# Digit comparisons stored by groups of four token columns, the first expert's high parts first, and a new plan, in a fused attention and routing kernel

## The chip, the cores and the metric

The program runs on one core of a Trainium2 chip. The metric is the device time of one execution in microseconds (us). Before the change it was 493.65 us as the median of three runs (492.44 to 495.6).

## The reference

Attention over 4 batches, 8 heads, 768 positions and 64 features: four sink keys and a window of 128, softmax, product with v. Its output is read as 3072 tokens of 512 features, and a greedy routing sends each token to one of 8 experts:

```python
cap = N // E                                   # 3072 / 8 = 384
logits = x @ w_gate
for idx in np.argsort(-logits.flatten()):      # best pairs first
    tok, e = idx // E, idx % E
    if assigned[tok] >= 0 or counts[e] >= cap: continue
    assigned[tok] = e; counts[e] += 1
for e in range(E):
    mask = assigned == e
    h = np.maximum(x[mask] @ w1[e], 0.0)       # 512 -> 1024
    out[mask] = h @ w2[e]                      # 1024 -> 512
```

Every expert gets exactly 384 tokens, and its MLP is done with float32 accuracy.

## The kernel before, in words

**Stages.** Attention takes the first 139 us, token columns of 128 tokens each (24 columns, NC=24). Then `Moe` runs eight rounds. Round k has a routing phase `Rk` (`phase`), which finds the expert that fills up next and its 384 tokens; a gather of these rows out of DRAM (`rows`, L683), which also transposes them on TensorE (L691) and splits them into a high part `xh` (ScalarE, L693) and a low part `xl` (VectorE, L694); the loading of the expert's 4 MB of weights as 8 pieces of 512 KB on SyncE's queue (`weights`, L674), each split into `wh` (ScalarE, L676) and `wl` (VectorE, L678); and the MLP (`mlp`).

**The MLP.** A product is made of three: high by high, high by low, low by high. Each of the 8 slices f of the hidden layer takes 4 x 3 matmuls of 384 columns (L704), then ScalarE and VectorE split the result into `hh` and `hl` (L707, L708). The second layer takes 3 x 8 x 3 matmuls of 512 columns (L716).

**A routing phase.** A token's best logit is turned into a sortable integer, and its digits are searched from the top in six steps (`STEPS`): two of 64 digit values (m=64), four of 32 (m=32). In a step VectorE compares the digits of all 24 columns with the m values (`compare`, L497, tile `cmp`), and TensorE counts per expert with one product for each group of columns: the weights are 128 columns of `cmp`, the moving operand is the one-hot `oh` (L567, 12 products of 128x16 for m=64, 6 of 128x32 for m=32). VectorE turns the counts into a digit (L584 to L589), one product with a constant matrix (L593) spreads it, VectorE takes the step's threshold from it (L595, L596), and the next step begins. After the six steps, ranks come from two products (L614, L615), and the tokens' indices from one more comparison and 12 products (`pick`, L640). The routing of round k+1 runs among the MLP products of round k; `R0` has nothing to run among. In `R0` and while the first rows are gathered, products with a constant (`warm`, L543) run in between.

**How `cmp` lies.** Before, a value of `cmp` is at `[digit value][token column]`: the 128 columns that one product loads as weights are `NC*m/128` elements apart, 12 elements (24 bytes) for m=64 and 6 elements (12 bytes) for m=32.

**What sets the order.** `graph` lists the work items with an engine and a cost, `order` is a list scheduler with one bias per class of items (`BIAS`: R, X, M, W and so on for each round) and a window (`WIN`), and `run` writes the instructions down in that order. Each engine works through its own list strictly in this order, so an item that is not ready holds back what stands behind it on its engine. The costs are the planner's own and set the order only.

Of the kernel before, what the change touches and what calls it, by code (L numbers as in the profile page):

```python
# [385 lines left out]
class Graph:  # L386
# [18 lines left out]
    def order(self,bias,win,free):  # L405
# [44 lines left out]
class Moe:  # L450
# [40 lines left out]
    def part(self,j,m): return self.cmp[j][:,0:m*NC].rearrange("p (x c) -> p x c",x=128)  # L491
    def compare(self,j,xb,m,a,b,op=OP.is_ge,dt=BF):

        V=self.nc.vector; g=128//m; h=NC//g
        o=self.part(j,m).bitcast(dt).rearrange("p (j m) c -> p j m c",j=g); x=xb.rearrange("p (j c) -> p j c",j=g)[:,:,None,:].to_broadcast([128,g,m,h])
        r=self.grid[:,None,0:m,0:h].to_broadcast([128,g,m,h])
        if (a,b)==(0,NC): V.tensor_tensor(o,x,r,op); return  # L497
        for i in range(g):
            c,d=max(a,i*h)-i*h,min(b,i*h+h)-i*h
            if c<d: V.tensor_tensor(o[:,i,:,c:d],x[:,i,:,c:d],r[:,i,:,c:d],op)  # L500
    def prep(self,k,a,b):

# [15 lines left out]
            (u(8*n),lambda: V.tensor_tensor(self.oh[:,c],w,wide(mx),OP.is_equal),'w1 mx','oh'),  # L518
            (u(32*n),lambda: self.compare(0,self.xb0,64,a,b),'xb0','cmp0'),
            (u(n/2),lambda: V.tensor_scalar(di[:,1],s,-2**31,15,op0=OP.bitwise_xor,op1=OP.logical_shift_right),'s','di1'),  # L520
# [24 lines left out]
    def phase(self,g,k):  # L545
# [7 lines left out]
        if not last:  # L553
# [79 lines left out]
        ip,bn=bank()  # L633
        v(u(NC*32),lambda: self.compare(oj,self.lo,64,0,NC,OP.is_equal,F16),'lo',on)
        v(u(6*NC),lambda: V.tensor_tensor(R,c4[:,:,0:6],c4[:,:,1:7],OP.subtract),'c40 c4','R')
        v(u(6*NC),lambda: V.tensor_tensor(self.R3,R,self.tid[:,:,None].to_broadcast([128,NC,6]),OP.mult),'R','R3')
        def pick():
            if first: self.warm(ip,WARM[6])
            OH=self.part(oj,64).bitcast(F16); h=NC//2
            for c in range(h): nc.tensor.matmul(ip[:,0:12],OH[:,:,c],self.R3.rearrange("p (j c) g -> p c j g",j=2)[:,c],start=c==0,stop=c==h-1)  # L640
        e(12*62*slow,pick,on+' R3',bn,'ip')

# [37 lines left out]
    def rows(self,g,k):  # L680
# [5 lines left out]
        for c in range(4):  # L686

            tp,tn=(self.py[c%2],f'py{c%2}') if k==0 and c>1 else (self.pt[c%2],f'pt{c%2}')
            pts=[tn,tn+'.1',tn+'.2']
            for t in range(3):  # L690
                g.add('E',110,lambda t=t,c=c,tp=tp: nc.tensor.transpose(tp[:,128*t:128*t+128],self.xg[t][:,128*c:128*c+128],self.idn),  # L691
                      [f'xg{t}'],[pts[t]],f'X{k}.{c}.{t}',f'X{k}')
            g.add('A',371,lambda c=c,tp=tp: nc.scalar.activation(self.xh[b][:,c,:],tp[:,0:CAP],AF.Copy),pts,[f'xh{b}.{c}'],f'xh{k}.{c}',f'X{k}')  # L693
            g.add('V',469,lambda c=c,tp=tp: nc.vector.tensor_tensor(self.xl[b][:,c,:],tp[:,0:CAP],self.xh[b][:,c,:].bitcast(F32),OP.subtract),pts+[f'xh{b}.{c}'],[f'xl{b}.{c}'],f'xl{k}.{c}',f'X{k}')  # L694

    def mlp(self,g,k):
        nc=self.nc; b=k%2; cls=f'M{k}'; idx=self.idx[k]
# [35 lines left out]
    def run(self):  # L733
# [113 lines left out]
```

## Time and profile before

| | |
|---|---|
| median of 3 runs | 493.65 us |
| the profiled execution | 495.15 us, span 493.4 us |
| TensorE matmuls busy | 454.1 us, 92% of the span |
| VectorE busy | 363.5 us, 74% |
| ScalarE / GpSimd busy | 225.5 us / 159.4 us |
| mean granted TensorE clock | 0.964 |

The profile is of one execution. Busy time counts an engine's instructions from first to last moment; matmuls are pipelined, so one matmul's duration is longer than the step from one start to the next. PEld stands for TensorE's weight loads, DVE for VectorE, ACT for ScalarE, POOL for GpSimd, SPq for SyncE's queue.

### The profile page before, as it was taken

Reading aid. Unit: us, or ns where it says so; the run is one execution under the profiler, and the core shown is the slowest. Engines: PE = TensorE matmul, PEld = TensorE weight load, DVE = VectorE, ACT = ScalarE, POOL = GpSimd, SP = SyncE. Lnnn points to the kernel's source line nnn. Section 1 sums busy time; section 2 is a strip of 40 time slices with the busy share of each in tenths; the row PEclk is TensorE's granted clock in tenths of the full one; section 3 lists DMA queues with packets and bytes.
Section 4 is the critical chain, followed back from the end, with each engine's and each line's share of the span. In section 5 each row is a group of like instructions: output and inputs, shape, how many; then the busy total and the mean of one; then the engine's idle time right before and its main releaser. Section 6 shows DMA issues by size and latency. Waiting matters only on the chain.

```text
span 493.4 us, 14321 instructions
## 1 busy us (share of the span) xinstructions
PE 454.1 (92%) x5572; PEld 377.8 (77%) x5572; DVE 363.5 (74%) x1168; ACT 225.5 (46%) x667; POOL 159.4 (32%) x322
## 2 busy tenths in 40 slices
PE   8799999988764989999999899999999999999994
PEld 4587877777632678788878778887988988998983
DVE  5799999989956877997888877986977764622010
ACT  5887888878300351541622442640632355612120
POOL 5877878767710300410320311201021303100011
PEclk9899999999955889999999999999999999999999
DMA  8766767752210570930922912902921995100011
GB/s 278 245 190 200 226 216 215 210 166 93 88 44 9 154 245 0 324 146 28 348 74 73 333 44 80 361 10 83 322 65 43 328 345 181 45 0 23 21 43 44
DMA packets 44452, 73.28 MB, mean 149 GB/s; under 512 B 3424, under 2 KB 20960, under 8 KB 44384
## 3 DMA queue, kind: packets, MB, share of 16 engines
q1 hardware_dynamic: 39968, 59.11, 36.2%
q0 software_dynamic: 3840, 12.59, 7.2%
q8 instruction: 44, 0.72, 0.6%
q10 hardware_dynamic: 576, 0.67, 0.5%
q14 instruction: 24, 0.20, 0.1%
HBM read 59.77 MB, written 12.58 MB: 147 GB/s over the span
## 4 chain that ended last, share of the span: by engine, by line
PE 57%; DVE 19%; DMA 9%; ACT 6%; issue 4%; POOL 2%; SPq 0%; POOLq 0%; ACTq 0%; DVEq 0%
PE py L716 22%; PE ph L704 20%; DMA raw<-w 7%; ACT P L24 4%; PE pp L83 3%; PE pr L567 3%; DVE nmx L95 2%; PE pp L132 2%; DVE wl L678 2%; PE pt L691 2%; DVE xt L149 2%; PE pp L112 2%; DVE at L139 1%; PE pp L143 1%; PE pp L145 1%
## 5 line engine op out<-in xcount | busy, mean ns | idle before, releaser
L676 ACT ACTIVATE wh<-raw 128x1024 fp32r<-128x1024 f32 x64 | 67.7, 1061 | 83.8 <-DVE fin L654 33.5
L678 DVE TENSOR_TENSOR wl<-raw,wh 128x1024 fp32r<-128x1024 f32 x64 | 77.4, 1217 | 27.4 <-ACT wh L676 27.0
L704 PE MATMUL ph<-xh,wh 128*128 128x384 f32 x256 | 90.7, 354 | 0.2 <-DVE hl L708 0.2
L704 PE MATMUL ph<-xl,wh 128*128 128x384 f32 x256 | 86.8, 339 | 0.0
L704 PE MATMUL ph<-xh,wl 128*128 128x384 f32 x256 | 86.8, 339 | 0.0
L683 POOL DMA_INDIRECT xg<-x_dram,idx x24 | 30.4, 1268 | 156.1 <-issue 37.8
L716 PE MATMUL py<-wh,hh 128*128 128x512 f32 x192 | 79.2, 413 | 0.0
L24 ACT ACTIVATE P<-pp,nmx 128x128 f32<-128x128 f32 x192 | 68.5, 379 | 16.1 <-DVE nmx L97 14.2
L716 PE MATMUL py<-wl,hh 128*128 128x512 f32 x192 | 75.4, 393 | 0.0
L716 PE MATMUL py<-wh,hl 128*128 128x512 f32 x192 | 75.4, 393 | 0.0
L721 POOL DMA_INDIRECT out<-yo,idx x24 | 24.9, 1037 | 137.0 <-ACT yo L719 122.7
L707 ACT ACTIVATE hh<-ph 128x384 fp32r<-128x384 f32 x64 | 30.7, 486 | 71.9 <-PE ph L704 55.3
L708 DVE SCALAR_TENSOR_TENSOR hl<-ph,hh 128x384 fp32r<-128x384 f32 x64 | 35.1, 552 | 30.3 <-ACT hh L707 29.5
L704 PEld LDWEIGHTS ph<-xh,wh 128*128 128x128 f32 x256 | 49.1, 192 | 5.6 <-issue 2.9
L704 PEld LDWEIGHTS ph<-xl,wh 128*128 128x128 f32 x256 | 48.7, 190 | 2.1 <-DVE xl L694 0.3
L704 PEld LDWEIGHTS ph<-xh,wl 128*128 128x128 f32 x256 | 48.5, 189 | 0.0
L83 PE MATMUL pp<-kk,q 64*64 64x204 f32 (+2 forms) x768 | 42.7, 333 | 3.5 <-ACT P L24 2.0
L716 PEld LDWEIGHTS py<-wh,hl 128*128 128x128 f32 x192 | 36.0, 188 | 8.1
L24 ACT ACTIVATION_READ_ACCUMULATOR P<-pp,nmx 128x1 f32 x192 | 41.7, 217 | 0.0
L716 PEld LDWEIGHTS py<-wh,hh 128*128 128x128 f32 x192 | 36.7, 191 | 6.1 <-issue 1.3
L118 POOL TENSOR_TENSOR E<-PT,me 128x256 f32<-128x256 f32 x48 | 35.4, 753 | 15.0 <-ACT PT L24 14.9
L716 PEld LDWEIGHTS py<-wl,hh 128*128 128x128 f32 x192 | 36.2, 189 | 4.3
(161 smaller groups left out, 794.9 us busy)
## 6 DMA issues: line engine op xcount, KB each, us to landing
raw<-w SPq DMA_DIRECT2D x64, 512.0 KB, 7.4
kk<-kd SPq DMA_DIRECT2D x23, 272.0 KB, 3.7
v<-vd SPq DMA_DIRECT2D x24, 256.0 KB, 3.1
x_dram<-xt SPq DMA_DIRECT2D x24, 256.0 KB, 3.4
q<-qd SPq DMA_DIRECT2D x22, 256.0 KB, 3.7
xg<-x_dram,idx POOLq DMA_INDIRECT x24, 6.0
out<-yo,idx POOLq DMA_INDIRECT x24, 2.7
us<-ud SPq DMA_DIRECT2D x1, 288.0 KB, 5.3
```

The costliest lines, as they stand in the source:

```text
L24: def act(*a,**k): last[:]=[nc.scalar.activation(*a,**k)]
L83: PE.matmul(sp[o,s,204*u+a:204*u+204],q[p,2*g+u,o],kk[p,2*i-2+f+a//68:2*i+f+1,2*g+u],start=True,stop=True)
L118: def op_A(c,g): G.tensor_tensor(T('E',c)[:,2*g:2*g+2],diag(c,g),me[:,None].to_broadcast([128,2,2,64]),OP.mult)
L567: nc.tensor.matmul(cnt[:,0:z*E],self.part(j,m)[:,:,c],self.oh.rearrange("p (j c) e -> p c j e",j=z)[:,c],start=c==0,stop=c==h-1)
L676: g.add('A',947,lambda wh=wh,raw=raw: nc.scalar.activation(wh,raw,AF.Copy),[f'raw{q}'],[f'wh{s}'],f'H{k}.{j}',f'W{k}')
L678: g.add(e,{'V':1160,'P':2303}[e],lambda wh=wh,wl=wl,raw=raw,e=e: (nc.vector if e=='V' else nc.gpsimd).tensor_tensor(wl,raw,wh.bitcast(F32) ...
L683: g.add('P',1350,lambda t=t: nc.gpsimd.indirect_dma_start(out=self.xg[t],out_offset=None,in_=self.x_dram,in_offset=bass.IndirectOffsetOnAx ...
L704: nc.tensor.matmul(p[:,0:CAP],x[:,c,:],y[:,c,:],start=c==0 and i==0,stop=c==3 and i==2)
L707: g.add('A',371,lambda f=f,p=p: nc.scalar.activation(self.hh[:,f,:],p[:,0:CAP],AF.Relu),ps,[f'hh{f}'],f'hh{k}.{f}',f'H{k}')
L708: g.add('V',469,lambda f=f,p=p: nc.vector.scalar_tensor_tensor(self.hl[:,f,:],p[:,0:CAP],0.0,self.hh[:,f,:].bitcast(F32),op0=OP.max,op1=OP ...
L716: nc.tensor.matmul(p,x[:,f,ts],w,start=f==0 and i==0,stop=f==7 and i==2)
L721: st=nc.gpsimd.indirect_dma_start(out=self.out,out_offset=bass.IndirectOffsetOnAxis(ap=idx[:,t:t+1],axis=0),in_=y,in_offset=None)
```

## The change

`RUN` gives the number of token columns in a group, 4 in all eight rounds. `compare` now writes `cmp` as `[group of 4][digit value][column in the group]`, so the columns that a product loads as weights are 4 elements (8 bytes) apart, and VectorE's operands run over 4 elements at a time. `gather` issues the products, for counting and for `pick` alike. For m=64 there are 12 products as before. For m=32 there are 8 in place of 6: four of 128 weights, and four of 64, as 24 columns make six groups and a product of 128 weights takes four of them. In the first round, slices 0 and 1 of the hidden layer take the eight matmuls with `xh` first and the four with `xl` at the end, and the counting of step 1 of `R1` is put behind the first two of these items (`m0go`). Costs of the planner, its window and all biases are new.

```diff
+RUN=[4]*8
...
-                if k and tiny: c+=90
+                if k and tiny: c+=15
...
-    def compare(self,j,xb,m,a,b,op=OP.is_ge,dt=BF):
+    def compare(self,j,xb,m,a,b,k,op=OP.is_ge,dt=BF):
-        V=self.nc.vector; g=128//m; h=NC//g
+        V=self.nc.vector; g=128//m; h=NC//g; U=RUN[k]
+        if U:
+            a//=U; b//=U; n=b-a
+            o=self.cmp[j][:,0:m*NC].bitcast(dt).rearrange("p (t m u) -> p t m u",m=m,u=U)[:,a:b]
+            x=xb[:,U*a:U*b].rearrange("p (t u) -> p t u",u=U)[:,:,None,:].to_broadcast([128,n,m,U])
+            V.tensor_tensor(o,x,self.grid[:,None,0:m,0:U].to_broadcast([128,n,m,U]),op); return
...
+    def gather(self,out,j,m,y,k,dt=BF):
+
+        z=128//m; U=RUN[k]; n=y.shape[2]; l=[]
+        if U:
+            for b in range(0,NC//U,z):
+                q=min(z,NC//U-b)
+                st=self.cmp[j][:,b*m*U:(b+q)*m*U].bitcast(dt).rearrange("p (x u) -> p u x",u=U); mv=y[:,b*U:(b+q)*U].rearrange("p (j u) e -> p u j e",u=U)
+                l+=[(q*m,q*n,st[:,u],mv[:,u]) for u in range(U)]
+        else:
+            st=self.part(j,m).bitcast(dt); mv=y.rearrange("p (j c) e -> p c j e",j=z)
+            l=[(128,z*n,st[:,:,c],mv[:,c]) for c in range(NC//z)]
+        l=[l[0]]+[x for x in l if x[0]<128]+[x for x in l[1:] if x[0]==128]
+        for i,(r,w,a,b) in enumerate(l): self.nc.tensor.matmul(out[0:r,0:w],a,b,start=i==0,stop=i==len(l)-1)
...
-                    for c in range(h):
-                        nc.tensor.matmul(cnt[:,0:z*E],self.part(j,m)[:,:,c],self.oh.rearrange("p (j c) e -> p c j e",j=z)[:,c],start=c==0,stop=c==h-1)
-                e(h*slow*62,counts,cn+' oh',bn,f'cnt{n}')
+                    self.gather(cnt,j,m,self.oh,k)
+                e({0:62*h if m==64 else 52*h,2:27*h,4:29*h if m==64 else 250}[RUN[k]]+(100 if first else 0),counts,cn+' oh'+(' m0go' if (k,n)==(1,1) else ''),bn,f'cnt{n}')
...
-                def mm(c=c,p=p,wh=wh,wl=wl):
+                def mm(c=c,p=p,wh=wh,wl=wl,two=k==0 and f<2):
+                    if two:
+                        for i,x in enumerate((wh,wl)): nc.tensor.matmul(p[:,0:CAP],x[:,c,:],self.xh[b][:,c,:],start=c==0 and i==0,stop=False)
+                        return
...
+            if k==0 and f<2:
+                for c in range(4): g.add('E',174,lambda c=c,p=p,wh=wh: nc.tensor.matmul(p[:,0:CAP],wh[:,c,:],self.xl[b][:,c,:],start=False,stop=c==3),[f'xl{b}.{c}',pn+('.3' if c==0 else f'.l{c-1}')],[pn+f'.l{c}'],f'Ml{f}.{c}',cls)
+                ps+=[pn+f'.l{c}' for c in range(4)]
...
-            if s-te>340 and te>=tr: ex.append((te+1,int((s-te-170)//165)))
+            if s-te>340 and te>=tr: ex.append((te+1,max(0,int((s-te-600)//165))))
...
-WIN=[33, 1401090, 1049]
+WIN=[110, 2865394, 2192]
...
```

The plan moves items on all engines. Three places are shown, the numbers of instructions left out.

TensorE, one counting of m=32 in `R0`, and the product that spreads its digit. Before:

```order
L567 MATMUL pr0_3339<-oh_106,cmp1_110 128x32
L567 LDWEIGHTS cmp1_110
L567 MATMUL pr0_3339<-oh_106,cmp1_110 128x32
L567 LDWEIGHTS cmp1_110
L567 MATMUL pr0_3339<-oh_106,cmp1_110 128x32
L593 LDWEIGHTS wt1_70
L593 MATMUL pr0_3339<-i81_112,wt1_70 128x8
```

The same place now:

```order
L519 MATMUL pr0_3338<-oh_106,cmp1_110 64x16
L519 LDWEIGHTS cmp1_110
L519 MATMUL pr0_3338<-oh_106,cmp1_110 64x16
L519 LDWEIGHTS cmp1_110
L519 MATMUL pr0_3338<-oh_106,cmp1_110 128x32
L519 LDWEIGHTS cmp1_110
L519 MATMUL pr0_3338<-oh_106,cmp1_110 128x32
L519 LDWEIGHTS cmp1_110
L519 MATMUL pr0_3338<-oh_106,cmp1_110 128x32
L611 LDWEIGHTS wt1_70
L611 MATMUL pr0_3338<-i81_112,wt1_70 128x8
```

Behind a first product of 128 weights come the four of 64 and then the other three of 128.

TensorE where the first MLP begins (`py1` holds the last transposed rows, `cmp1` is step 1 of `R1`). Before:

```order
L567 MATMUL pr0_3339<-oh_106,cmp1_110 128x16
L691 MATMUL py1_3338<-idt_62,xg2_3322 128x128
L704 MATMUL ph0_3334<-xh0_3323,wh0_3296 128x384
L704 MATMUL ph0_3334<-xl0_3325,wh0_3296 128x384
L704 MATMUL ph0_3334<-xh0_3323,wl0_3308 128x384
```

Now:

```order
L708 MATMUL py1_3337<-idt_62,xg2_3321 128x128
L721 MATMUL ph0_3333<-xh0_3322,wh0_3295 128x384
L721 MATMUL ph0_3333<-xh0_3322,wl0_3307 128x384
L721 MATMUL ph0_3333<-xh0_3322,wh0_3295 128x384
L721 MATMUL ph0_3333<-xh0_3322,wl0_3307 128x384
L721 MATMUL ph1_3334<-xh0_3322,wh0_3295 128x384
L721 MATMUL ph1_3334<-xh0_3322,wl0_3307 128x384
L519 LDWEIGHTS cmp1_110
L519 MATMUL pr0_3338<-oh_106,cmp1_110 128x16
```

The 12 countings of step 1 have gone from in front of the last transposed rows to behind six matmuls of the MLP.

VectorE around step 2 of `R1`, between its comparison and its digit `i81`, on which TensorE's L593 (now L611) waits. Before:

```order
L497 TENSOR_TENSOR cmp0_109<-xb0_103,grid_66 128x768
L576 SCALAR_TENSOR_TENSOR y_96<-x0_101,df_108 128x24
L678 TENSOR_TENSOR wl2_3310<-raw2_3290,wh2_3298 128x1024
L584 TENSOR_SCALAR odd_113<-pr0_3339 64x16
L678 TENSOR_TENSOR wl3_3311<-raw3_3291,wh3_3299 128x1024
L585 TENSOR_TENSOR two_114<-pr0_3339,odd_113 64x16
L588 TENSOR_SCALAR odd_113<-two_114 32x8
L678 TENSOR_TENSOR wl4_3312<-raw4_3292,wh4_3300 128x1024
L589 SCALAR_TENSOR_TENSOR i81_112<-two_114,odd_113 32x8
```

Now (`wl2` stands three instructions ahead of the first row):

```order
L500 TENSOR_TENSOR cmp0_109<-xb0_103,grid_66 128x768
L594 SCALAR_TENSOR_TENSOR y_96<-x0_101,df_108 128x24
L732 SCALAR_TENSOR_TENSOR hl0_3327<-ph0_3333,hh0_3326 128x384
L695 TENSOR_TENSOR wl3_3310<-raw3_3290,wh3_3298 128x1024
L602 TENSOR_SCALAR odd_113<-pr0_3338 64x16
L732 SCALAR_TENSOR_TENSOR hl0_3327<-ph1_3334,hh0_3326 128x384
L603 TENSOR_TENSOR two_114<-pr0_3338,odd_113 64x16
L695 TENSOR_TENSOR wl4_3311<-raw4_3291,wh4_3299 128x1024
L606 TENSOR_SCALAR odd_113<-two_114 32x8
L695 TENSOR_TENSOR wl5_3312<-raw5_3292,wh5_3300 128x1024
L607 SCALAR_TENSOR_TENSOR i81_112<-two_114,odd_113 32x8
```

Before, the comparison stood ahead of `wl2` and the digit behind `wl4`; now the comparison stands behind `wl2` and the digit behind `wl5`.

## Rows read from the trace of the kernel before

**Rows 1.** The page: busy time of TensorE, and its granted clock in 40 slices.

```profile
PE 454.1 (92%) x5572; PEld 377.8 (77%) x5572; DVE 363.5 (74%) x1168; ACT 225.5 (46%) x667; POOL 159.4 (32%) x322
...
PEclk9899999999955889999999999999999999999999
```

**Rows 2.** Stretches: start and end, length, busy time by engine, granted clock, DMA.

```profile
139.00:161.00 22.00, 10.88 (x82) 5.77 (x83) 14.41 (x80) 0.00 (x0) 0.67 (x3) 0.50 0.09 28
...
178.00:181.00 3.00, 0.58 (x5) 0.35 (x4) 2.14 (x6) 2.09 (x4) 0.00 (x0) 1.00 1.01 382
181.00:184.20 3.20, 3.20 (x17) 2.89 (x17) 2.71 (x8) 2.93 (x4) 0.00 (x0) 0.51 0.12 44
...
340.00:380.00 40.00, 40.00 (x252) 34.61 (x252) 32.14 (x116) 14.34 (x21) 5.84 (x6) 1.00 0.44 151
```

**Rows 3.** Chain of waits in `R0`: start, length, what.

```profile
143.47 0.91 DVE cmp L497
...
144.43 0.88 PE pr L567 x12
...
160.04 0.84 PE pr L640 x12
```

**Rows 4.** Timeline of TensorE inside trains: start, length, engine, line, operation, count.

```profile
168.03 0.38 PE L567 MATMUL pr<-oh,cmp 128*128 128x16 bf16 x4
...
174.82 0.34 PE L567 MATMUL pr<-oh,cmp 128*128 128x32 bf16 x4
...
197.18 0.20 PE L614 MATMUL pr<-M,ltf 128*128 128x48 bf16 x1
...
197.22 0.18 PE L615 MATMUL pr<-sc,onesb 128*128 128x48 bf16 x1
...
197.25 0.49 PE L716 MATMUL py<-wh,hh 128*128 128x512 f32 x1
```

**Rows 5.** Costliest groups: busy us, mean ns of one, idle before.

```profile
L704 PEld LDWEIGHTS ph<-xh,wl 128*128 128x128 f32 x256 | 48.5, 189 | 0.0
...
L83 PEld LDWEIGHTS pp<-kk,q 64*64 64x64 f32 x768 | 25.2, 134 | 9.6 <-ACT P L24 2.8 <-DMA q<-qd 1.4 <-ACT PT L24 0.8
L567 PE MATMUL pr<-oh,cmp 128*128 128x16 bf16 (+1 forms) x336 | 25.1, 204 | 4.2 <-DVE cmp L497 2.6 <-DVE di L523 1.3
```

**Rows 6.** Timeline of VectorE: comparisons of three sizes in `R0`.

```profile
141.49 0.44 DVE L500 TENSOR_TENSOR cmp<-xb,grid 128x192 bf16<-128x192 bf16 x1
...
143.41 0.96 DVE L497 TENSOR_TENSOR cmp<-xb,grid 128x1536 bf16<-128x1536 bf16 x1
...
146.36 0.56 DVE L497 TENSOR_TENSOR cmp<-xb,grid 128x768 bf16<-128x768 bf16 x1
```

**Rows 7.** Waits of TensorE from 171 us on: total us, times, longest.

```profile
PE pr L593 <- DVE i L589: 3.5, 3, 2.4
PE pr L567 <- DVE cmp L497: 1.2, 2, 0.7
```

**Rows 8.** Timeline of TensorE around its longest wait in the first MLP.

```profile
177.91 0.33 PE L704 MATMUL ph<-xl,wh 128*128 128x384 f32 x1
178.09 0.34 PE L704 MATMUL ph<-xh,wl 128*128 128x384 f32 x1
180.84 0.17 PE L593 MATMUL pr<-i,wt 128*128 128x8 bf16 x1 [2.42 <-DVE i L589]
...
181.15 0.52 PE L704 MATMUL ph<-xl,wh 128*128 128x384 f32 x1
181.47 0.52 PE L704 MATMUL ph<-xh,wl 128*128 128x384 f32 x1
```

**Rows 9.** Timeline of VectorE in the same stretch.

```profile
175.63 1.23 DVE L678 TENSOR_TENSOR wl<-raw,wh 128x1024 fp32r<-128x1024 f32 x1 [1.14 <-ACT wh L676]
...
179.50 1.23 DVE L678 TENSOR_TENSOR wl<-raw,wh 128x1024 fp32r<-128x1024 f32 x1 [0.79 <-ACT wh L676]
180.64 0.15 DVE L589 SCALAR_TENSOR_TENSOR i<-two,odd 32x8 bf16<-32x8 f32 x1
```

**Rows 10.** Timeline of ScalarE: the high parts of weight pieces 4 and 5.

```profile
178.41 1.06 ACT L676 ACTIVATE wh<-raw 128x1024 fp32r<-128x1024 f32 x1 [1.35 <-DMA raw<-w]
...
180.72 1.06 ACT L676 ACTIVATE wh<-raw 128x1024 fp32r<-128x1024 f32 x1 [0.50 <-DMA raw<-w]
```

More of the change, by code (lines that the diff above doesn't have):

```diff
@@ L518, in prep @@
             (u(8*n),lambda: V.tensor_tensor(self.oh[:,c],w,wide(mx),OP.is_equal),'w1 mx','oh'),
-            (u(32*n),lambda: self.compare(0,self.xb0,64,a,b),'xb0','cmp0'),
+            (u((32,32,64,32,32)[RUN[k]]*n),lambda: self.compare(0,self.xb0,64,a,b,k),'xb0','cmp0'),
             (u(n/2),lambda: V.tensor_scalar(di[:,1],s,-2**31,15,op0=OP.bitwise_xor,op1=OP.logical_shift_right),'s','di1'),
@@ L561, in phase @@
                 cnt,bn=bank(); j=n%2; cn=f'cmp{j}'; z=128//m; h=NC//z
-                if n: v(u(NC*m/2),lambda j=j,m=m: self.compare(j,xb[j],m,0,NC),f'xb{j}',cn)
+                if n: v(u(NC*m/(1 if RUN[k]==2 else 2)),lambda j=j,m=m: self.compare(j,xb[j],m,0,NC,k),f'xb{j}',cn)
                 def counts(n=n,m=m,cnt=cnt,z=z,h=h,j=j):
                     if first: self.warm(cnt,WARM[n])
-                    for c in range(h):
-                        nc.tensor.matmul(cnt[:,0:z*E],self.part(j,m)[:,:,c],self.oh.rearrange("p (j c) e -> p c j e",j=z)[:,c],start=c==0,stop=c==h-1)
-                e(h*slow*62,counts,cn+' oh',bn,f'cnt{n}')
+                    self.gather(cnt,j,m,self.oh,k)
+                e({0:62*h if m==64 else 52*h,2:27*h,4:29*h if m==64 else 250}[RUN[k]]+(100 if first else 0),counts,cn+' oh'+(' m0go' if (k,n)==(1,1) else ''),bn,f'cnt{n}')
                 if n:
@@ L633, in phase @@
         ip,bn=bank()
-        v(u(NC*32),lambda: self.compare(oj,self.lo,64,0,NC,OP.is_equal,F16),'lo',on)
+        v(u(NC*(64 if RUN[k]==2 else 32)),lambda: self.compare(oj,self.lo,64,0,NC,k,OP.is_equal,F16),'lo',on)
         v(u(6*NC),lambda: V.tensor_tensor(R,c4[:,:,0:6],c4[:,:,1:7],OP.subtract),'c40 c4','R')
@@ L638, in pick @@
             if first: self.warm(ip,WARM[6])
-            OH=self.part(oj,64).bitcast(F16); h=NC//2
-            for c in range(h): nc.tensor.matmul(ip[:,0:12],OH[:,:,c],self.R3.rearrange("p (j c) g -> p c j g",j=2)[:,c],start=c==0,stop=c==h-1)
-        e(12*62*slow,pick,on+' R3',bn,'ip')
+            self.gather(ip,oj,64,self.R3,k,F16)
+        e({0:740,2:310,4:350}[RUN[k]]+(100 if first else 0),pick,on+' R3',bn,'ip')
         r2=ip[:,0:12].rearrange("p (j t o) -> p j t o",j=2,o=2); sw=self.sw
@@ L690, in rows @@
             for t in range(3):
-                g.add('E',110,lambda t=t,c=c,tp=tp: nc.tensor.transpose(tp[:,128*t:128*t+128],self.xg[t][:,128*c:128*c+128],self.idn),
+                g.add('E',98,lambda t=t,c=c,tp=tp: nc.tensor.transpose(tp[:,128*t:128*t+128],self.xg[t][:,128*c:128*c+128],self.idn),
                       [f'xg{t}'],[pts[t]],f'X{k}.{c}.{t}',f'X{k}')
@@ L701, in mlp @@
             for c in range(4):
-                def mm(c=c,p=p,wh=wh,wl=wl):
+                def mm(c=c,p=p,wh=wh,wl=wl,two=k==0 and f<2):
+                    if two:
+                        for i,x in enumerate((wh,wl)): nc.tensor.matmul(p[:,0:CAP],x[:,c,:],self.xh[b][:,c,:],start=c==0 and i==0,stop=False)
+                        return
                     for i,(x,y) in enumerate(((wh,self.xh[b]),(wh,self.xl[b]),(wl,self.xh[b]))):
                         nc.tensor.matmul(p[:,0:CAP],x[:,c,:],y[:,c,:],start=c==0 and i==0,stop=c==3 and i==2)
-                g.add('E',522,mm,[f'wh{s}',f'wl{s}',f'xh{b}.{c}',f'xl{b}.{c}']+([pn if c==1 else pn+f'.{c-1}'] if c else []),[pn] if c==0 else [pn+f'.{c}'],f'M{k}.{f}.{c}',cls)
+                two=k==0 and f<2
+                g.add('E',348 if two else 522,mm,[f'wh{s}',f'wl{s}',f'xh{b}.{c}']+([] if two else [f'xl{b}.{c}'])+([pn if c==1 else pn+f'.{c-1}'] if c else []),([pn] if c==0 else [pn+f'.{c}'])+(['m0go'] if (k,f,c)==(0,0,1) else []),f'M{k}.{f}.{c}',cls)
             ps=[pn]+[pn+f'.{c}' for c in (1,2,3)]
+            if k==0 and f<2:
+                for c in range(4): g.add('E',174,lambda c=c,p=p,wh=wh: nc.tensor.matmul(p[:,0:CAP],wh[:,c,:],self.xl[b][:,c,:],start=False,stop=c==3),[f'xl{b}.{c}',pn+('.3' if c==0 else f'.l{c-1}')],[pn+f'.l{c}'],f'Ml{f}.{c}',cls)
+                ps+=[pn+f'.l{c}' for c in range(4)]
             g.add('A',371,lambda f=f,p=p: nc.scalar.activation(self.hh[:,f,:],p[:,0:CAP],AF.Relu),ps,[f'hh{f}'],f'hh{k}.{f}',f'H{k}')
```

2 lines of the change are left out of this document (1 added, 1 removed).

## Prediction

> **What bounds the kernel now.** I read the busy times and the granted clock first [rows 1], then the stretches [rows 2], then the chain of waits in `R0` [rows 3], then TensorE's waits behind it [rows 7], and last the timeline inside the trains of small products [rows 4]. The reader is to see two different kernels. From 139 to 161 us, in `R0`, TensorE is busy half the time at half the clock [rows 2], and the end is set by a chain that hands from VectorE to TensorE and back; a train of 12 counting products takes 0.88 us of it, the train of `pick` 0.84 us [rows 3]. From the first MLP on, TensorE is the bound: 40.00 of 40 us are busy from 340 to 380 us [rows 2], and from 171 us on its waits sum to 4.7 us, all on a routing phase's digit or comparison [rows 7]. There, what a train loses or gains on TensorE comes out of the time nearly one to one. One place is worse than its wait: after 2.4 us without work at 178 us [rows 8] the granted clock is 0.51 for the next 3.2 us, though it was 1.00 up to then [rows 2].
>
> **The change, part by part.** *Spacing of the weights.* Inside a train, four starts at 24 bytes between weight columns span 0.38 us, so one step is (0.38 - 0.204)/3 = 0.059 us, with 204 ns for the last product itself; at 12 bytes it is (0.34 - 0.204)/3 = 0.045 us [rows 4, 5]. Two products whose constant weights lie side by side follow each other, and are followed, within 0.04 and 0.03 us [rows 4], 0.035 on the mean. No row has 8 bytes. The ends are 0.045 (no better than 12 bytes) and 0.030. [...]
>
> [...]
>
> A train of 12 has 11 steps, so it gives back 11 x (0.059 - 0.031) = 0.31 us. From the first MLP on there are 18 of them on TensorE (two in `R1`, three each in `R2` to `R6`, one in `R7`): **5.5 us**. Two more lie on the chain of `R0` (step 1 and `pick`): **0.6 us**. Step 0 of `R0` is mostly done under attention and counts for nothing; if that cover were gone it would cost 0.3 us.
>
> *m=32: eight products for six.* Before, 5 steps of 0.045 = 0.23 us; now 7 steps of 0.031 = 0.22 us. Over 28 trains (24 in `R1` to `R6`, 4 in `R0`) that is **-0.3 us**. The other end, 0.045 a step, is +2.5 us.
>
> *The comparisons.* Even runs of 12 and of 6 elements cost the same: 1536 elements take 0.96 and 768 take 0.56 us, so 0.40 us for 768; a run of three, 192 elements, takes 0.44 us [rows 6]. Runs of four are even, so I take the same rate and no change for the large ones. The last columns of `R0` are now 256 elements in an even run, 0.56 - 512 x 0.40/768 = 0.29 us in place of 0.44: **-0.15 us** on the chain. The other end, half the rate, is a rival below.
>
> *High parts first.* Work is moved, not removed: the train of step 1 of `R1` goes from ahead of the MLP to inside it. The MLP starts earlier by that train and by the wait for the first low parts, and does the train later. Its cover is the weights: pieces 4 and 5 arrive so late that ScalarE starts on them at 178.41 and 180.72 us [rows 10], and VectorE behind it. I cost it at **-0.1 us**, between 0 and -0.6.
>
> *The first MLP in the new order.* Before, `wl4` ran from 179.50 us, the digit of step 2 followed at 180.64 [rows 9], and L593 with all of the MLP behind it waited from 178.09 to 180.84 [rows 8]. Now the digit stands behind `wl5` too: by the same rows ScalarE ends piece 5 at 181.78 [rows 10], `wl5` takes 1.23 more, and the digit comes at 183.0. But TensorE has more MLP products ahead of that L593 now, and it first has to wait for step 2's comparison, which now stands behind `wl2` (from 175.63 for 1.23 us [rows 9]). So I see two waits of about one microsecond in place of one of 2.4: the sum stays, what is late next is again a weight piece, but no stretch is long enough to be followed by the low clock. At half clock a matmul of 384 columns took 0.32 us where it took 0.18 [rows 8]; of the 3.2 us at 0.51 [rows 2] half is given back, **-1.6 us**. Ends: 0 and -1.6 for the clock, -2.4 and +2.4 for the waits.
>
> *The rest of the plan.* The small waits in rounds 2 and 3 (the 2.3 us left of rows 7) may go or double; the tail behind the last product is the same list of instructions. I take **0**, within 2.3 either way.
>
> **Sum:** -5.5 - 0.6 - 0.3 - 0.15 - 0.1 - 1.6 = -8.25 us. The profiled execution took 495.15 us, 1.5 above the median of the runs, 493.65; its span 493.4 leaves 1.75 around it, which stays. Its own sum is 486.9; against the median, which is what will be compared, it is 485.4. **Forecast 485.5 us.**
>
> **The rivals.** *More.* The new order also removes three quarters of TensorE's waits of rows 7, 3.5 us: 481.9 us. For it: two of them are in rounds whose order is new; against it: in the first MLP I read waits again. Chance 0.12.
>
> *Eight bytes bring little.* The excess over side-by-side weights could shrink with the distance alone: 0.024 at 24 bytes, 0.010 at 12, some 0.007 at 8. Then a step is 0.042, trains of 12 give 20 x 11 x 0.017 = 3.7, and m=32 loses 28 x (7 x 0.042 - 0.23) = 1.8: 493.65 - 3.7 + 1.8 - 0.15 - 0.1 - 1.6 = 489.9 us. Chance 0.13. The change would not do what it says.
>
> *Short weights load slowly.* Half as many columns may not load faster: float32 weights of 128 columns take 189 ns, of 64 columns 134 [rows 5], so 64 columns cost 55 ns there. If the four products of 64 step at 0.055, a train for m=32 takes 3 x 0.031 + 4 x 0.055 = 0.31 us, 0.08 more than before: 28 x 0.08 = +2.2 in place of -0.3, and the time is 487.9 us. For it: the change makes such products where there were none; against it: no row has 16-bit weights of 64 columns. Chance 0.10. [...]
>
> *The waits take it back.* If the digit of step 2 is waited for in one piece until 183.0, the clock falls as before and the first MLP gains nothing but the 0.1; if the other waits double too (+2.3), the time is 485.4 + 1.6 + 2.3 = 489.3 us. Chance 0.12.
>
> *Slower: the comparisons lose half their rate.* [...] On the chain of `R0` that is 2 x 0.80 + 4 x 0.40 = 3.2 us in full. In `R1` to `R6` it is 3 x 0.8 + 4 x 0.4 = 4.0 each, 24 in all, of which MLP products cover part; at half of it the time is 485.4 + 3.2 + 12 = 500.6 us. It decides (over 498.6) once some 10 of the 24 us show. Against it: 12 and 6 elements cost the same rate; for it: three did not. Chance 0.06.
>
> **How the numbers follow.** The forecast itself, from 482.5 to 488, has 0.47. About 1%, 4.9 us, is what a measurement of this kernel can tell from no change. Faster by over 1% is below 488.7: the forecast, "more" and about half of the short weights, 0.64. Slower by over 1% is above 498.6: the comparisons and a plan that fits badly somewhere, 0.09. The rest is 0.27. The range takes in the middle rivals and most of "more", 480.5 to 493.
>
> **What would show it.** Right: in the new trace, steps of some 0.031 us inside the trains of 12, which then span some 0.55 us in place of 0.84 to 0.88; comparisons still 0.96 and 0.56 us; granted clock 1.00 from the first MLP on; TensorE's waits on L611 and L519 no more than 4.7 us. Wrong: steps of 0.045 and up, trains for m=32 above 0.3 us, comparisons above 1 us, a low clock at the first MLP (it is kept up by fewer `warm` products now), or a new wait of several microseconds in a later round, where a weight piece stands ahead of a digit on VectorE.

## The result, and the profile after

The changed kernel takes 502.62 us (median of four runs, 500.15 to 504.48), the one before beside it 494.62 us: ratio 1.0145, 95% interval 1.0102 to 1.0187. It is slower, by some 7 to 8 us, where the forecast was 485.5. The profiled execution took 504.48 us and is the longest of the four.

The page of the changed kernel: busy time, and TensorE's granted clock in 40 slices. They answer to [rows 1].

```profile
PE 457.7 (91%) x5621; PEld 379.6 (76%) x5621; DVE 364.0 (72%) x1167; ACT 225.0 (45%) x667; POOL 159.7 (32%) x322
...
PEclk9899999999975899959999999999999999999998
```

TensorE is busy for 3.6 us longer, in 49 products more, though its trains of 12 are shorter. In the clock, the 15th slice (from 173 us before, 176 us now) went from 8 to 9, and the 18th (from 214 us) fell from 9 to 5.

Stretches of the changed kernel, with the columns of [rows 2]: TensorE's busy time is the first after the length, the granted clock the third number from the end.

```profile
172.00:178.00 6.00, 5.75 (x44) 5.00 (x41) 4.99 (x13) 3.50 (x6) 0.00 (x0) 1.00 0.80 269
178.00:184.00 6.00, 5.43 (x34) 4.68 (x33) 4.93 (x10) 4.75 (x8) 0.00 (x0) 1.00 0.70 258
208.00:212.00 4.00, 4.00 (x19) 3.13 (x18) 3.65 (x10) 2.53 (x3) 0.99 (x1) 1.00 1.06 403
212.00:216.00 4.00, 1.57 (x18) 1.04 (x17) 2.77 (x5) 1.54 (x2) 0.99 (x1) 0.94 1.04 384
216.00:220.00 4.00, 2.15 (x14) 1.26 (x13) 2.73 (x12) 0.81 (x3) 0.44 (x1) 0.50 0.40 147
220.00:224.00 4.00, 3.68 (x20) 3.34 (x21) 3.46 (x11) 2.92 (x6) 0.54 (x1) 0.50 0.19 70
```

The first MLP (172 to 184 us) runs at full clock, as forecast, and TensorE pauses in it for 0.8 us in all where two waits of about one were forecast. The long wait and the low clock stand 35 us later instead: from 212 to 220 us TensorE works 3.7 of 8 us, and it is at half clock from 216 us on.

The timeline of TensorE in the changed kernel: a train of the 64-value step in `R0`, one of a 32-value step, and the products around the long wait.

```profile
145.44 0.56 PE L519 MATMUL pr<-oh,cmp 128*128 128x16 bf16 x12 [0.42 <-DVE cmp L500]
...
187.33 0.75 PE L519 MATMUL pr<-oh,cmp 128*128 128x32 bf16 x8
...
212.74 0.56 PE L519 MATMUL pr<-oh,cmp 128*128 128x16 bf16 x12
213.16 0.41 PE L708 MATMUL pt<-idt,xg 128*128 128x128 f32 x2
216.84 0.17 PE L611 MATMUL pr<-i,wt 128*128 128x8 bf16 x1 [3.26 <-DVE i L607]
```

The train of 12 in `R0` takes 0.56 us, 0.32 less than before [rows 3]. But the train of eight is 0.75 us, and each of the 28 is like it (0.72 to 0.79). Six products of before take 0.45 (a row below shows such a train).

VectorE in the changed kernel: the comparisons of two sizes, which answer to [rows 6], and its work during that wait.

```profile
144.42 0.96 DVE L500 TENSOR_TENSOR cmp<-xb,grid 128x1536 bf16<-128x1536 bf16 x1
...
212.76 1.21 DVE L695 TENSOR_TENSOR wl<-raw,wh 128x1024 fp32r<-128x1024 f32 x1
214.00 0.17 DVE L606 TENSOR_SCALAR odd<-pr 64x8 f32<-64x8 f32 x1
215.37 1.22 DVE L695 TENSOR_TENSOR wl<-raw,wh 128x1024 fp32r<-128x1024 f32 x1 [1.20 <-ACT wh L693]
216.62 0.16 DVE L607 SCALAR_TENSOR_TENSOR i<-pr,odd 64x8 bf16<-64x8 f32 x1
...
217.46 0.56 DVE L500 TENSOR_TENSOR cmp<-xb,grid 128x768 bf16<-128x768 bf16 x1
```

The comparisons cost what they did. Routing's digit `i` had its first half (`odd`) at 214.00, but a low part of a weight piece stands between, and that one waits for ScalarE:

```profile
214.28 1.06 ACT L693 ACTIVATE wh<-raw 128x1024 fp32r<-128x1024 f32 x1 [2.47 <-DMA raw<-w]
```

ScalarE waits 2.47 us for the transfer of the piece. So a transfer holds VectorE's queue, that holds `i`, and `i` holds TensorE's whole queue. Waits of TensorE in the changed kernel from 165 us on (total, times, longest), which answer to [rows 7]:

```profile
PE pr L519 <- DVE cmp L500: 4.3, 4, 2.2
PE pr L611 <- DVE i L607: 4.1, 4, 3.3
```

They are 8.4 us where they were 4.7. By themselves they do not make this kernel slower than the one before: an experiment below has as much of them and takes 491 us.

### The profile page after: what moved, and what is told of

Its sections match the earlier page's. It is cut to its first block, busy times and chain, and to the rows that moved or that the text cites. A ratio compares the mean times of both kernels' runs of the same rounds, so it can differ in the third digit from the quotient of the medians.

```text
span 502.7 us, 14432 instructions
## 1 busy us (share of the span) xinstructions
PE 457.7 (91%) x5621; PEld 379.6 (76%) x5621; DVE 364.0 (72%) x1167; ACT 225.0 (45%) x667; POOL 159.7 (32%) x322
## 5 line engine op out<-in xcount | busy, mean ns | idle before, releaser
L724 PE MATMUL ph<-xh,wh 128*128 128x384 f32 x248 | 88.6, 357 | 0.6 <-DVE hl L732 0.6
L745 POOL DMA_INDIRECT out<-yo,idx x24 | 27.1, 1131 | 184.7 <-ACT yo L743 125.5
L724 PE MATMUL ph<-xl,wh 128*128 128x384 f32 x248 | 84.1, 339 | 0.0
L724 PE MATMUL ph<-xh,wl 128*128 128x384 f32 x248 | 84.1, 339 | 0.0
L700 POOL DMA_INDIRECT xg<-x_dram,idx x24 | 28.2, 1173 | 116.7 <-issue 74.6
L724 PEld LDWEIGHTS ph<-xh,wh 128*128 128x128 f32 x248 | 47.6, 192 | 3.1 <-DVE hl L732 0.9
L724 PEld LDWEIGHTS ph<-xl,wh 128*128 128x128 f32 x248 | 47.3, 191 | 1.8
L724 PEld LDWEIGHTS ph<-xh,wl 128*128 128x128 f32 x248 | 47.1, 190 | 0.0
L519 PEld LDWEIGHTS <-cmp 128*128 128x128 bf16 (+2 forms) x488 | 27.9, 126 | 23.8 <-DVE cmp L500 15.6
```

Of the source, the lines that this page charges most:

```text
L519: for i,(r,w,a,b) in enumerate(l): self.nc.tensor.matmul(out[0:r,0:w],a,b,start=i==0,stop=i==len(l)-1)
L700: g.add('P',1350,lambda t=t: nc.gpsimd.indirect_dma_start(out=self.xg[t],out_offset=None,in_=self.x_dram,in_offset=bass.IndirectOffsetOnAx ...
L745: st=nc.gpsimd.indirect_dma_start(out=self.out,out_offset=bass.IndirectOffsetOnAxis(ap=idx[:,t:t+1],axis=0),in_=y,in_offset=None)
```

## The experiments

Each ratio compares a kernel with runs of the kernel before on the same chip, whose own medians lie between 492.3 and 494.7 us, so two rows are compared by their ratios and not by their medians; one per cent is 4.9 us, and a difference of two ratios is uncertain by 0.4 to 0.7%, 2 to 3.5 us. Single executions of one kernel differ by up to 8 us, so sizes come from the ratios, and profiles, of one execution each, are used for places and durations.

| kernel | median, us | ratio to before | 95% interval |
|---|---|---|---|
| the change | 502.62 | 1.0145 | 1.0102 to 1.0187 |
| old plan, all of the new storage | 499.46 | 1.016 | 1.0103 to 1.0217 |
| old plan, new storage for 64 values alone | 492.3 | 0.9977 | 0.9937 to 1.0017 |
| new plan, new storage for 64 values alone | 491.03 | 0.998 | 0.9946 to 1.0014 |
| new plan, 32-value steps with eight wide loads | 491.39 | 0.998 | 0.9945 to 1.0015 |
| new plan, old storage | 496.5 | 1.0097 | 1.0066 to 1.0128 |
| the change, widths alternating | 512.33 | one run | |
| planned anew with measured costs, 1 | 489.41 | 0.993 | 0.9894 to 0.9965 |
| planned anew with measured costs, 2 | 491.08 | 0.9971 | 0.9934 to 1.0008 |

Theory W: in the 32-value steps the weights change between 128 and 64 columns, and that makes them long. Theory P: the new plan made the slowdown.

### The storage alone, in the old plan

```diff
+RUN=[4]*8
...
-    def compare(self,j,xb,m,a,b,op=OP.is_ge,dt=BF):
+    def compare(self,j,xb,m,a,b,k,op=OP.is_ge,dt=BF):
...
+                    self.gather(cnt,j,m,self.oh,k)
```

The bodies are those of the change; costs, biases and order are of before. 

> The kernel before with its own plan and order, and of the change only the new storage (groups of four columns for the 64-value and the 32-value steps, with the four products of 64 weight columns). Theory W (widths: going between weights of 128 and of 64 columns makes each of the 28 trains of 32-value steps 0.31 us longer, 0.46 to 0.77): +8.7 for these, -6.1 for the 20 trains of 64-value steps and picks (0.28 each, five of ten of R0's part on the path at most), so 494.6 + 2.5 = 497 (495.5 to 498.5). Theory P (the plan: the new order's waits made the slowdown, and the trains' length is hidden or paid back): the storage alone gains what was forecast for it, 488 (486.5 to 490).

Measured: ratio 1.016, +7.9 us: slower without the new plan. This is more than W expected (+2.5), because the gain of the 64-value trains, which W took off, is missing; the next run shows that.

### New storage for the 64-value steps alone, in the old plan

```diff
-        V=self.nc.vector; g=128//m; h=NC//g; U=RUN[k]
+        V=self.nc.vector; g=128//m; h=NC//g; U=RUN[k] if m==64 else 0
...
-        z=128//m; U=RUN[k]; n=y.shape[2]; l=[]
+        z=128//m; U=RUN[k] if m==64 else 0; n=y.shape[2]; l=[]
```

> The kernel before with its own plan and order, the new storage for the 64-value steps and the pick alone; the 32-value steps as before (6 products, 12 bytes). Theories W and P agree on 494.6 - 5.5 - 0.6 = 488.5 (487.5 to 490). If what a shorter train saves is waited away at the next step of routing: 492 to 494.6.

Measured: ratio 0.9977, -1.1 us, with an interval of -3.1 to +0.8. Against the run above, the 32-value steps' new storage costs 1.016 - 0.9977 = 1.8%, 9.0 us: W's 8.7. But of the 5 to 6 us that the 64-value trains give back, about one arrives, as in the last case of the expectation. The timelines of TensorE and VectorE at one of the 18 places, before:

```profile
240.63 0.84 PE L567 MATMUL pr<-oh,cmp 128*128 128x16 bf16 x12
...
243.21 0.17 PE L593 MATMUL pr<-i,wt 128*128 128x8 bf16 x1 [0.23 <-DVE i L589]
```

```profile
240.41 0.17 DVE L647 TENSOR_TENSOR idx<-pr,sw 64x3 int32<-64x3 f32 x1
240.61 0.56 DVE L708 SCALAR_TENSOR_TENSOR hl<-ph,hh 128x384 fp32r<-128x384 f32 x1
241.08 1.22 DVE L678 TENSOR_TENSOR wl<-raw,wh 128x1024 fp32r<-128x1024 f32 x1
242.33 0.17 DVE L588 TENSOR_SCALAR odd<-pr 64x8 f32<-64x8 f32 x1
242.53 0.56 DVE L708 SCALAR_TENSOR_TENSOR hl<-ph,hh 128x384 fp32r<-128x384 f32 x1
243.00 0.15 DVE L589 SCALAR_TENSOR_TENSOR i<-pr,odd 64x8 bf16<-64x8 f32 x1
```

And the same two engines at the same place with the short trains:

```profile
238.26 0.54 PE L519 MATMUL pr<-oh,cmp 128*128 128x16 bf16 x12
...
240.84 0.17 PE L611 MATMUL pr<-i,wt 128*128 128x8 bf16 x1 [0.56 <-DVE i L607]
```

```profile
238.05 0.16 DVE L664 TENSOR_TENSOR idx<-pr,sw 64x3 int32<-64x3 f32 x1
238.24 0.56 DVE L725 SCALAR_TENSOR_TENSOR hl<-ph,hh 128x384 fp32r<-128x384 f32 x1
238.72 1.22 DVE L695 TENSOR_TENSOR wl<-raw,wh 128x1024 fp32r<-128x1024 f32 x1
239.97 0.17 DVE L606 TENSOR_SCALAR odd<-pr 64x8 f32<-64x8 f32 x1
240.16 0.56 DVE L725 SCALAR_TENSOR_TENSOR hl<-ph,hh 128x384 fp32r<-128x384 f32 x1
240.64 0.15 DVE L607 SCALAR_TENSOR_TENSOR i<-pr,odd 64x8 bf16<-64x8 f32 x1
```

The train is 0.30 us shorter and the wait behind it 0.33 longer. VectorE works from `idx` to `i` with no pause, 2.59 us from start to start in both kernels; the train was hidden beside that. This gives a further theory, V: what TensorE saves at such places is waited away, because a digit stands behind VectorE's own long work or behind a low part that waits for its transfer.

### New storage for the 64-value steps alone, in the new plan

The same two lines, in the changed kernel. 

> The changed kernel with its plan and order, but the 32-value steps stored as before (6 products of 128 weight columns, 12 bytes). Theory W: 28 x 0.31 = 8.7 come off 502.6, so 494 or less (490 to 495; at the lower end the waits of TensorE behind the long trains go too). Theory P: the waits of the order stay and the trains' length was not what set the end, so 499 to 502.6.

Measured: ratio 0.998, -1.0 us to before. To the change it is 1.0145 - 0.998 = 1.65%, 8.2 us less. W's expectation holds and P's does not: without the new 32-value trains the change is not slower than the kernel before. TensorE's waits from 165 us on are no smaller than in the change, 8.8 us, and the long one is there too:

```profile
PE pr L611 <- DVE i L607: 6.9, 6, 3.3
PE pr L519 <- DVE cmp L503: 1.9, 3, 0.8
```

### Eight products, all with 128 weight columns

```diff
-                q=min(z,NC//U-b)
+                q=min(z,NC//U-b); w=b-(z-q)
-                st=self.cmp[j][:,b*m*U:(b+q)*m*U].bitcast(dt).rearrange("p (x u) -> p u x",u=U); ...
+                st=self.cmp[j][:,w*m*U:(b+q)*m*U].bitcast(dt).rearrange("p (x u) -> p u x",u=U); ...
-                l+=[(q*m,q*n,st[:,u],mv[:,u]) for u in range(U)]
+                l+=[((z-q)*n,z*n,st[:,u],mv[:,u]) for u in range(U)]
...
+        for i,(r,w,a,b) in enumerate(l): self.nc.tensor.matmul(out[:,r:w],a,b,start=i==0,stop=i==len(l)-1)
```

> The changed kernel with its plan, order and storage, 8 products in a 32-value step, all eight with weights of 128 columns: the last four load the columns of groups 2 to 5 and multiply the moving columns of groups 4 and 5 into the half of the outputs that needs them not zeroed; the widths of weights never change. It leaves out the right summing of these outputs where rows of groups 2 and 3 meet columns of groups 4 and 5, which routing does not read. Theory W: trains of 0.2 + 8 x 0.033 = about 0.46, so the time of a_m64 within 1 us (490 to 495). Theory N (number of products or the 8 bytes make a 32-value train long, not the widths): trains stay near 0.77 and the time near 502.

Measured: ratio 0.998, the time of the run above. A train of a 32-value step, in the timelines of TensorE of three kernels: eight wide products, then six wide products as of before (new plan, new storage for 64 values alone), then the widths alternating (next experiment); the changed kernel's own is the row at 187.33 above, 0.75.

```profile
183.29 0.43 PE L518 MATMUL pr<-oh,cmp 128*128 128x32 bf16 x8
```

```profile
183.12 0.45 PE L519 MATMUL pr<-oh,cmp 128*128 128x32 bf16 x6
```

```profile
187.10 1.16 PE L519 MATMUL pr<-oh,cmp 128*128 128x32 bf16 x8
```

So the two products more, at 8 bytes, cost nothing and bring nothing; nor is it the moving operand, as four of the eight still move 16 columns, like the narrow ones. By the starts in the trace the seven steps of the wide train are 55, 34, 31, 32, 33, 35 and 33 ns, together 253; six products of 12 bytes take 255. In the changed kernel (train at 187.33) they are 135 into the first narrow weights, 83, 62 and 60 between narrow ones, 136 back to wide ones, 57 and 34: 567 ns, 0.31 us more.

### Widths alternating

```diff
-        l=[l[0]]+[x for x in l if x[0]<128]+[x for x in l[1:] if x[0]==128]
+        l=[l[i] for i in (0,4,1,5,2,6,7,3)] if m==32 and U else l
```

> The changed kernel, its eight products of a 32-value step in the order wide, narrow, wide, narrow, wide, narrow, narrow, wide: 6 changes of the width of the weights instead of 2, the same eight products. Theory W (each change of width costs a step of about 0.137 us where one between narrow ones is 0.060 and between wide ones 0.035): six steps of 0.137 and one of 0.060, first to last start about 0.88 us instead of 0.57, so 28 x 0.31 = 8.7 more, some 511. Rival N (it is the four narrow loads that cost, each some 0.08 more, wherever they stand): 0.57 and the time of the changed kernel, 502 in an undisturbed run.

Measured: 512.33 us, and the train above of 1.16 us, whose steps are 136, 159, 135, 160, 140, 81 and 139 ns: six changes of width of 135 to 160, and one step of 81 between narrow weights. W foretold 0.88 us from first to last start and its rival 0.57; it is 0.95. Two prices add up: a change of width costs some 100 to 125 ns over a wide step, a narrow load after a narrow one 25 to 50. In the changed kernel's train the first is about 0.2 us of the 0.31, the second the rest.

### The new plan alone

```diff
-RUN=[4]*8
+RUN=[4]*8; LAY=[0]*8
...
-        V=self.nc.vector; g=128//m; h=NC//g; U=RUN[k]
+        V=self.nc.vector; g=128//m; h=NC//g; U=LAY[k]
```

(and the same in `gather`). 

> The changed kernel's plan, order and first expert's high parts first, with the old storage in all of routing's steps (its costs in the plan kept, so the order is the same): what the new plan does alone. From the run with the old storage of the 32-value steps alone (491.0) add back 20 trains of 64-value steps: +5.7 where TensorE's time sets the end, so 496.5; nearer 492 if the order leaves these trains waits to hide in, as the plan of before does.

Measured: ratio 1.0097, +4.8 us (interval +3.3 to +6.3). With the old storage the new plan, high parts first included, is slower. From it, the 64-value storage takes off 1.0097 - 0.998 = 1.2%, 5.8 us, about what was forecast for it. But with the 64-value storage in both, the two plans take the same time (0.998 and 0.9977), and with all of the new storage too, within the uncertainty (1.0145 and 1.016). So, as measured, the plan's cost and the worth of the 64-value trains are no fixed numbers: each depends on the other. Two stretches, of the kernel before and of this one:

```profile
172.00:184.00 12.00, 9.58 (x56) 8.43 (x55) 9.62 (x24) 7.36 (x10) 0.00 (x0) 0.88 0.76 263
208.00:220.00 12.00, 11.83 (x77) 9.61 (x76) 11.37 (x28) 6.39 (x10) 3.05 (x3) 1.00 0.49 182
```

```profile
172.00:184.00 12.00, 11.64 (x71) 10.40 (x70) 10.48 (x25) 8.27 (x11) 0.00 (x0) 1.00 0.54 197
208.00:220.00 12.00, 8.42 (x56) 6.90 (x55) 9.59 (x29) 6.24 (x9) 1.22 (x2) 0.72 0.52 195
```

What the first MLP gains, 2.1 us of work and the clock, is lost again at 208 to 220 us: 3.4 us of work, and the clock at 0.72. There the plan has used up the first expert's second layer before the second expert's tokens are transposed; in the kernel before, matmuls of that layer stand between the transposes. This profile is of the shortest of that kernel's six executions (493.26 us, where the profile of before has 495.15). So it shows one stretch that became worse, not where the 4.8 us are lost: that stays open. In the five profiles of kernels with this plan TensorE's wait here is 2.2 to 3.3 us; with the old plan no wait from 208 to 220 us is above 0.5.

### Does VectorE's load or the transfers take the gain back?

Three pairs, each with the old plan: once with the old storage, once with the new one for 64 values. In the first, VectorE does less: from the 13th weight piece on it computes half of the low part.

```diff
-            g.add(e,...,lambda wh=wh,wl=wl,raw=raw,e=e: (nc.vector if e=='V' else nc.gpsimd).tensor_tensor(wl,raw,wh.bitcast(F32),OP.subtract),
+            g.add(e,...,lambda wh=wh,wl=wl,raw=raw,h=512 if n>=self.NW else 1024: nc.vector.tensor_tensor(wl[:,0:h],raw[:,0:h],wh[:,0:h].bitcast(F32),OP.subtract),
```

> The kernel before with less work for VectorE: from the 13th of the 64 weight blocks on, the low part of the weights is computed for the left 512 of its 1024 columns only (the right half keeps the low part of an older block, so the low products are not those of the reference). By the rows of 1024 and of 384 columns (1.217 and 0.552 us) one costs about 0.69 instead of 1.22 us; 52 of them take some 28 us off VectorE, nothing off TensorE. Theory D (after the first MLP TensorE waits for routing's operations because VectorE is late with them): the 6.2 us of waits shrink to 1 to 3, and the time to 487 to 490. Rival S (these waits are not VectorE's load): 491 to 493.

> The same lighter VectorE (the low part of later weight blocks for half of the columns only) with the new storage of the 64-value steps and the pick. Theory D: the 5.7 us that TensorE's shorter trains save, of which no more than 1 us or so reached the time beside the full VectorE, now reach it: 5 to 6 below the run with the lighter VectorE alone, 482 to 484. Rival S (the saving is lost in something else than waits on VectorE): 0 to 2 below that run.

In the second, half of each weight piece is loaded from the ninth on (`n` is the piece's number):

```diff
+                    u=4 if n<self.NR else 2
+                    src=self.w1[bass.ds(ei,1),0:128*u,256*j:256*j+256]...
```

> The kernel before with half of the weight transfers: from the 9th of the 64 blocks on, only the left half of a block is loaded (256 KB instead of 512; the right half keeps older weights, so the output is not the reference's), all else is done in full. Theory F (VectorE's queue is in order and the low part of a weight block often stands ahead of routing's operation that TensorE waits for; that low part waits for ScalarE's high part, and this for the transfer): ScalarE's 34 us of waits on transfers nearly go, TensorE's 6.2 us of waits shrink to 2 or 3, the time to 487 to 490. Rival S: no change, 492 to 493.

> Half of the weight transfers as in the run beside it, with the new storage of the 64-value steps and the pick. Theory F: with the blocks early, what the shorter trains save reaches the time, 5 to 6 below the run beside it (482 to 484). Rival S (the saving is lost in something else than the arrival of weights): 1 to 2.5 below it, as with the full transfers and with the lighter VectorE.

In the third, both:

> The kernel before with both reliefs: half of the weight transfers from the 9th block on, and from the 13th block on the low part for half of the columns (the output is not the reference's). Theory V (TensorE's waits for routing come from VectorE's order: its own long low part in some places, a low part that waits for its transfer in others, so one relief alone only hands the wait to the other): both together take most of the waits away, 486 to 489 where either alone gave 491. Rival S: 490 to 491.

> Both reliefs, with the new storage of the 64-value steps and the pick. Theory V: the trains' 5.7 us now reach the time, 4.5 to 6 below the run beside it (481 to 484). Rival S (most of that saving is lost elsewhere than in waits on VectorE's order): 1 to 2.5 below it, as with the full work and with either relief alone.

| relief | old storage: us, ratio, interval | 64 values new: us, ratio, interval | difference of the ratios |
|---|---|---|---|
| none | | 492.3, 0.9977, 0.9937 to 1.0017 | 0.23%, 1.1 us |
| VectorE lighter | 491.2, 0.9965, 0.9932 to 0.9997 | 488.9, 0.9922, 0.9892 to 0.9951 | 0.43%, 2.1 us |
| half the transfers | 490.88, 0.9946, 0.9917 to 0.9976 | 488.49, 0.992, 0.9886 to 0.9953 | 0.26%, 1.3 us |
| both | 490.2, 0.9911, 0.9872 to 0.9951 | 484.95, 0.9836, 0.9788 to 0.9883 | 0.75%, 3.7 us |

Either relief alone failed its expectations: with the old storage 487 to 490 us was expected, and of the shorter trains 5 to 6 us, where 2.1 and 1.3 came. With both, the old storage took 490.2 us, in the rival's range and not in V's; of the shorter trains 3.7 us come by the ratios and 5.2 by the medians, where V expected 4.5 to 6 and the rival 1 to 2.5. As a difference of two ratios is uncertain by up to 0.6% here, the times alone do not tell 3.7 us from 1.1. (The 6.2 us of waits that two expectations give the kernel before are 4.7 in its profile [rows 7]; with the short trains they are 6.3.)

The profiles say more. The waits of TensorE from 165 us on, with the short trains and no relief, with VectorE lighter, with half the transfers, and with both:

```profile
PE pr L611 <- DVE i L607: 4.6, 6, 2.2
PE pr L519 <- DVE cmp L500: 1.7, 3, 1.2
```

```profile
PE pr L611 <- DVE i L607: 3.9, 3, 2.2
PE pr L519 <- DVE cmp L500: 0.7, 2, 0.5
```

```profile
PE pr L611 <- DVE i L607: 4.8, 7, 2.3
PE pr L519 <- DVE cmp L500: 0.7, 3, 0.3
```

```profile
PE pr L611 <- DVE i L607: 0.7, 1, 0.7
PE pr L519 <- DVE cmp L500: 0.5, 2, 0.3
```

The longest wait in each is that of the first MLP. Behind it, from 184 us on, the waits on a digit or a comparison are 4.0, 2.1, 3.0 and 0.3 us, and 2.3 in the kernel before. So in these profiles VectorE's work and the transfers take turns as the last to arrive, as V says; but the last profile is of the shortest of its six executions (479.81 us). The short trains with no relief brought 1.7 us of waits, 4.0 against 2.3, where 4 to 5 us are missing: V is shown at the places looked at and as a part of the loss, and the rest of it stays open.

### Planned anew with what the trains take

The change's plan counts 0.25 us for a 32-value train and 0.35 for a 64-value one. By the starts in the trace, from the first product of a train to the one behind it, they take TensorE 0.30 us (old storage) and 0.42. Two tables of biases, and windows, were searched for at 0.31 and 0.41, with the old storage for 32 values:

```diff
-                e({0:62*h if m==64 else 52*h,2:27*h,4:29*h if m==64 else 250}[RUN[k]]+...
+                e((410 if m==64 else 310)+...
...
-WIN=[110, 2865394, 2192]
+WIN=[5, 2865394, 102]
```

> The changed kernel with the old storage for the 32-value steps, and planned with what its trains take (0.41 us for a 64-value train, 0.31 for a 32-value one; the change's plan had 0.35 and 0.25), by a table of biases searched for with transfers up to 0.9 us late. The planner's own sum is 3.5 us below the changed plan's at these costs: 491 - 3.5 = 487.5 (486 to 490) if the plan's waits are what is left to gain; 490 to 492 if waits are set by what the plan does not know.

> As the run beside it, its biases searched for from those of the kernel before. The planner's sum is 1.3 us above that of the run beside it: 488.8 (487 to 491); 491 to 493 if waits are set by what the plan does not know.

Measured: 489.41 us, ratio 0.993 (0.9894 to 0.9965), and 491.08 us, 0.9971 (0.9934 to 1.0008). The first beats both kernels, by 3.5 us and by some 10 us, and lies in its expected range (486 to 490); the second lies at the upper edge of its own (487 to 491). Against the change's plan with the same storage (0.998) the first gains 0.5%, which is within the uncertainty, and what the costs did and what the search did is not told apart. The long wait at 213 us is gone from it; in its first MLP waits of 3.2 and 1.1 us are left over:

```profile
PE ph L724 <- DVE hl L732: 4.3, 2, 3.2
PE pr L519 <- DVE cmp L503: 1.5, 2, 1.1
```

## Why the prediction was wrong

- **Spacing, 64 values (-5.5 and -0.6).** The size was right: a train goes from 0.84 to 0.88 us [rows 3] to 0.56, 0.28 to 0.32 against 0.31 forecast. No row of before shows the 0.031 us of a step that the sum is made with; it lies near the lower of its two ends, that of side-by-side weights. In the changed kernel's trace a step is mostly 31 to 35 ns by the starts (the train at 212.74 has 56 first, then 31 to 34), where it was about 60. That the train's gain "comes out of the time nearly one to one" fits the new plan (5.8 us between two runs), and failed in the old one (1.1 us): the prediction took a busy TensorE for the bound everywhere, and did not look at what VectorE was doing beside a train.
- **m=32 (-0.3).** This is the step that failed, and without it the change would not be slower: +8.2 us instead of -0.3 (1.0145 against 0.998), and +9.0 in the old plan. The prediction priced all seven steps between the eight products as steps between 128 weight columns. The rival "short weights load slowly" named the right place and gave it 0.10, but priced only the load (55 ns, from another data type's rows) and not the change of width, which no row of before showed: 0.08 us a train where 0.31 was measured. In the traces a step between loads of 64 columns took 60 to 83 ns (the train at 187.33), one between loads of 128 mostly 31 to 35 (the wide train).
- **Comparisons.** Right: 0.96 and 0.56 us, as in [rows 6], and 0.29 for the last columns of `R0`; the rival on them fell.
- **The first MLP (-1.6), high parts first (-0.1).** Right on the clock, 1.00 from 172 to 184 us. Of the `warm` products ahead of it there are fewer, 25 in a row from 162.37 us where 33 ran from 160.72; the clock was 1.00 from 168 to 172 us, with TensorE busy for 3.79 of the 4. The waits there are other ones than forecast, and shorter: 0.6 us on `hl` and 0.3 on `xh`, not about one each on step 2's comparison and digit.
- **The rest of the plan (0, within 2.3).** Mis-sized: plan and high parts together measured +4.8 with the old storage, where -1.7 was forecast, and +0.1 with the 64-value storage in both plans. Either way, of 64-value trains and plan together about 1 us arrived (0.998) where some 8 were forecast. The prediction looked for waits at the places of before; the new plan made one where there had been none, at 213 us, of the kind that it named as the sign of failure, and behind it the clock was 0.50 for 8 us.
- **The sum.** The forecast had -8.25, measured is +7.2 (the ratio's 1.0145 on 494.6). The steps +4.8 - 5.8 + 8.2 add up to it because each starts at the kernel where the last one ends, so this is no check of them. Of the 15.4 us between, 8.5 are the trains for m=32 and 7 the gain of the 64-value trains and of the plan that did not arrive. The range, to 493, took in the rival on short weights at its own price, 487.9; at the measured 0.31 us a train, 28 x 0.31 = 8.7 in place of -0.3, the forecast alone would have been 494.5. "Slower by over 1%", with a plan that fits badly as one of its two reasons, had 0.09.

## What to carry to other kernels

Keep the weights of a train of small matmuls at one width: here it was cheaper to load 64 columns that another product needs than to load 64 fewer (0.43 us a train against 0.75). A train that is shortened beside another engine's work, as at 240 us above (0.30 us shorter, the wait behind it 0.33 longer), gains only what that engine leaves open, so look at what the next waited-for operation stands behind in its queue before the saving is counted. And when a plan is made anew with guessed costs, look at the new order for a stretch where the filler has run out, not only at the waits of the old one.

## What the runs showed of the hardware

- With bf16 weights, 8 bytes between their columns, and at full clock, a step from 128 to 64 weight columns or back took some 135 to 160 ns in the trains shown, one between loads of 64 took 60 to 83, one between loads of 128 mostly 31 to 35 (the first of a train, and the first after a change of width, some 55).
- After some 3.3 us in which TensorE did nothing at 213 us, the granted clock was 0.50 from 216 to 224 us, though TensorE was busy for 3.68 of the last 4 us of it; after waits of 0.6 and 0.3 us in the first MLP it stayed at 1.00.
- VectorE's comparison took the same time in runs of 4 elements as in longer ones: 1536 elements 0.96 us in runs of 12 and of 4, 768 elements 0.56 us in runs of 6 and of 4.
